# Retention followed by routed experts on one core: transposes spread between the products, and weight pieces issued ahead of the first scatter

## The chip, the cores and the metric

One core of a Trainium2 chip. The metric is the device time of one execution in microseconds; a run is one execution, and the figure for a kernel is the median of its runs.

## The reference

```python
# q, k, v: (4, 8, 768, 64); x has N = 3072 rows of D = 512; 8 experts, F = 1024
gamma = 1.0 - 2.0 ** (-5.0 - np.arange(H))
for t in range(S):
    state = gamma * state + einsum('bhd,bhe->bhde', k[:, :, t], v[:, :, t])
    y[:, :, t] = scale * einsum('bhd,bhde->bhe', q[:, :, t], state)
x = y.transpose(0, 2, 1, 3).reshape(N, D)

do_compute = x @ w_skip > 0          # rows that are not computed stay x
e_idx = argmax(xc @ w_gate)          # one expert for each row
gate_w = softmax(xc @ w_gate)[e_idx]
y[mask] = gate_w[mask] * (relu(xc[mask] @ w1[e]) @ w2[e])
out[do_compute] = xc + y
```

## The kernel before

Instructions run on each engine in the order in which the program writes them; the tile framework adds the waits. There are two stages.

**Attention.** The work is cut into 16 pairs, i = 0 to 15: one batch and two heads each. load(i) brings q, k and v of a pair (384 KB each) on SP's queue, three buffers for q and k, five for v. scaled_q and scaled_k multiply by powers of gamma on POOL. t_q and t_k transpose the scaled tiles on TensorE (six 128x128 transposes each), and ACT copies the result out of PSUM as QT and KT. s_at(i, r) forms the products of QT and KT for each half of the rows (24 small products), and DVE masks them into ATm. s_kv(i) forms k'v for each chunk (40 products), and DVE adds them up into the prefix sums Z. s_inter(i) multiplies QT by Z (20 products) and s_av(i) adds ATm times v (48 products) in the same PSUM tile; ACT copies it as xT. t_x(i) transposes it back (six transposes) into xall, and stores(i) writes finished rows to out on ACT's queue. One turn of the loop holds steps of different pairs: t_q(i+1), t_k(i+1), t_x(i-2), then s_inter(i-1), s_at(i, 0), s_kv(i), s_av(i-1), s_at(i, 1).

The PSUM tiles are: "P", two buffers of two banks, for t_q, s_at, t_x and all gate tiles; "KV", one buffer, for t_k and s_kv; "Y", one buffer, for s_inter and s_av.

Between these the router runs for a finished batch, one part in each turn: gates_pe(i) on TensorE (logits with the gate columns Wc; their transpose; counts; the table of slots) and gates_dve(i) on DVE (choice of the expert, values, positions, one-hot rows). Wc holds the gate's and the skip's columns; it is zeroed and then loaded by two small DMAs on SP.

The weights of the experts come as 64 pieces of 256 KB (fp32 in HBM, bf16 in SBUF), issued by POOL through give(n). Experts 0 to 3 are brought during the attention (list `quota`), experts 4 to 7 (32 pieces) afterwards, when the attention's memory is free.

**Experts.** A task is an expert and one or two tiles of 128 slots. gather brings the rows of a tile from out (indirect DMA on POOL), cast makes bf16 on DVE, turn transposes (four transposes) into xgT, layer1 runs 32 products with ACT's relu into hT, layer2 runs 8 products for each tile, DVE forms yo, and POOL scatters it to out. The first tiles of experts 0 to 3 can be gathered before the last batch is routed (SL[0]); the second tiles need SL[1]. Behind the head, ten tasks run in a loop: (2), (3), the second tiles of 0 to 3, then experts 4 to 7 with both tiles (n = 6 to 9). In turn n: layer1(n), turn(n+1), cast(n+2), layer2(n), gathers, give(3). A G_.drain() stands behind task n = 7. At the end a loop for experts with more than 256 rows runs npass times, here 0.

```python
    give(5)
    ha, pe = g_pick(g_turn(Gs))
    cast(0, [0])
    turn(0, [0])
    h0 = layer1(0, [0])
    cp = g_count(B - 1, ha)
    g_vals(B - 1, ha, pe)
    g_pos(B - 1, g_mine(ha, cp))
    cast(1, [0])
    turn(1, [0])
    layer2(0, h0, [0], SL, True)
    slot_table(one_hots(poolC, chunks(B - 1), [1]), chunks(B - 1), [1])
```

Of the kernel before, what the change touches and what calls it, by code (L numbers as in the profile page):

```python
# [9 lines left out]
FP32 = mybir.dt.float32  # L10
# [8 lines left out]
def kernel(  # L19
# [95 lines left out]
    def scaled_q(i, eng=G_):  # L115
        scaled(i, qs, qw, tq, "qs", 2, eng)
# [4 lines left out]
    for r in range(R):  # L121
        for hi in range(2):
            G_.affine_select(
                out=maskc[64 * hi : 64 * hi + 64, r, :], in_=maskc[64 * hi : 64 * hi + 64, r, :],
                pattern=[[1, C]], base=-r, channel_multiplier=-R, compare_op=ALU.is_ge, fill=0.0,
            )
    scaled_q(0, V_)
    scaled_k(0)
    load(2)

# [20 lines left out]
    def give(n):  # L151
        for _ in range(n):
            if pieces:
                piece_w(*pieces.pop(0))
# [15 lines left out]
    def t_k(i):  # L170
        if i >= NU:
            return
        KT[i] = poolR.tile([128, R, G, 128], FP32, tag="KT", bufs=2, name="KT")
        ps = psR.tile([128, 2, 512], FP32, tag="KV", bufs=1, name="ktps")
        turned(ps, ks[i])
        A_.copy(out=KT[i][:, :, :, :].rearrange("p r g t -> p r (g t)"), in_=ps[:, :, 0 : G * 128])
# [281 lines left out]
    def chunks(b):  # L458
        return list(range(b * NCH, (b + 1) * NCH))
# [31 lines left out]
    for i in range(NU + 1):  # L491
        scaled_q(i + 1)
        scaled_k(i + 1)
        if i == 0:
            s_at(0, 0)
            s_kv(0)
            s_at(0, 1)
            t_q(1)
            t_k(1)
        else:  # L500
            t_q(i + 1)
            t_k(i + 1)
            t_x(i - 2)
            stores(i)
            gates_pe(i)
            s_inter(i - 1)
            s_at(i, 0)
            s_kv(i)
            s_av(i - 1)
            s_at(i, 1)  # L510
            gates_dve(i)
        if i == 1:
# [27 lines left out]
            Wc = poolC.tile([128, NDB, 32], FP32, name="Wc")  # L540
            V_.memset(Wc[:, :, :], 0.0)
            with nc.allow_non_contiguous_dma(reason="gate columns"):
                SP.dma_start(out=Wc[:, :, 0:E], in_=moe_w_gate.rearrange("(a p) e -> p a e", p=128))
                SP.dma_start(out=Wc[:, :, E : E + 1], in_=moe_w_skip.rearrange("(a p o) -> p a o", p=128, o=1))
# [41 lines left out]
    def turn(e, sts):  # L586
        xgT[e] = poolE.tile([128, NDB, CAP], BF16, tag="xgT", bufs=3, name="xgT")
        for s in sts:
# [6 lines left out]
            V_.tensor_copy(  # L595
# [53 lines left out]
    give(5)  # L649
    psE = ctx.enter_context(tc.tile_pool(name="pse", bufs=1, space=bass.MemoryType.PSUM, reuse_waits="tile"))  # L650
    ha, pe = g_pick(g_turn(Gs))
    cast(0, [0])
    turn(0, [0])
    h0 = layer1(0, [0])
    cp = g_count(B - 1, ha)
    g_vals(B - 1, ha, pe)
    g_pos(B - 1, g_mine(ha, cp))
    cast(1, [0])
    turn(1, [0])
    layer2(0, h0, [0], SL, True)  # L660
    slot_table(one_hots(poolC, chunks(B - 1), [1]), chunks(B - 1), [1])
    SL[1] = slots(poolC, 1, "b")
    h0 = layer1(1, [0])
    cast(2, [0])
    turn(2, [0])
    layer2(1, h0, [0], SL, True)
    cast(3, [0])
    g_sum(B - 1, ha)
    cn = g_count_all()
    NPASS = (N + CAP - 1) // CAP - 1  # L670
    thr_i = poolC.tile([128, NPASS], I32, name="thr_i")
    G_.iota(thr_i[:, :], pattern=[[CAP, NPASS]], base=CAP, channel_multiplier=0)
    thr = poolC.tile([128, NPASS], FP32, name="thr")
    V_.tensor_copy(thr[:, :], thr_i[:, :])
    top = poolC.tile([128, 1], FP32, name="top")
    V_.tensor_reduce(out=top[:, :], in_=cn[:, 0, 0:E], axis=AXX, op=ALU.max)
    V_.tensor_scalar(thr[:, :], thr[:, :], top[:, 0:1], None, ALU.is_lt)
    npass = poolC.tile([128, 1], FP32, name="npass")
    V_.tensor_reduce(out=npass[:, :], in_=thr[:, :], axis=AXX, op=ALU.add)
    npass_i = poolC.tile([128, 1], I32, name="npass_i")  # L680
    V_.tensor_copy(npass_i[:, :], npass[:, :])
# [11 lines left out]
    for n, (e, sts) in enumerate(tasks):  # L693
# [8 lines left out]
        if n == len(tasks) - 3:  # L702
            G_.drain()
# [46 lines left out]
```

## Time and profile before

| | |
|---|---|
| median of 3 runs | 261.31 us (259.85 to 266.01) |
| the profiled execution | 260.44 us, span 258.7 us |
| PE busy | 202.4 us (78%), 3536 products |
| weight loads (PEld) busy | 161.9 us (63%) |
| DVE, ACT, POOL busy | 99.5, 77.3, 118.5 us |
| granted TensorE clock, mean | 0.94 |
| DMA moved | 49.83 MB, mean 193 GB/s |

The span runs from the first to the last instruction of the profiled execution; the time beside it has what lies around. Times in rows are microseconds from the span's start. Busy PE is not PE at its peak, since products are pipelined. In a timeline a row is a run of like instructions: its start, the time from the first's start to the last's end, the engine (an engine with q is its sequencer), the line, what is written and read, how many, and in brackets how long the engine had been idle before and what ended that. "issue" is idle time that the profile puts down to nothing that it shows.

### The profile page before, as it was taken

To read this page: it belongs to the slowest core of one execution; us is meant where nothing else is said; L and a number is where in the kernel's file an instruction comes from. 1 tells how busy PE (TensorE), PEld (TensorE's weight loads), DVE (VectorE), ACT (ScalarE), POOL (GpSimd) and SP (SyncE) were. 2 spreads that over 40 slices of the span, in tenths; PEclk is the share of its full clock that TensorE was granted. 3 is DMA by queue.
4 is the path that set the end of the run, shared out by engine and by line. 5 is a ranking of instruction groups with operands and counts; after the bars stand their busy time and mean duration, and the time that the engine had idled before them with its cause. 6 is when DMAs were issued, how large, how long until landed. Compare 5 with 4: busy or idle time off the path is not lost. (4 is left out here: it accounts for less than half of the span.)

```text
span 258.7 us, 8104 instructions
## 1 busy us (share of the span) xinstructions
PE 202.4 (78%) x3536; PEld 161.9 (63%) x3536; DVE 99.5 (38%) x304; ACT 77.3 (30%) x139; POOL 118.5 (46%) x146
## 2 busy tenths in 40 slices
PE   1899499977978966989795885887789999868080
PEld 1689389766877865879594763654457667626020
DVE  3135314334584243684135654344233514140020
ACT  2254144513522431543242222211224233303000
POOL 4672345552364165076290028013788787350411
PEclk9999979999999999999999998578999999997957
DMA  7991999969998988984989968920699999964611
GB/s 202 291 238 13 262 288 262 277 211 250 197 243 186 244 228 233 258 215 82 172 173 215 225 196 245 195 65 31 163 200 232 237 263 238 258 131 78 123 50 37
DMA packets 54520, 49.83 MB, mean 193 GB/s; under 512 B 3802, under 2 KB 42202, under 8 KB 54480
## 3 DMA queue, kind: packets, MB, share of 16 engines
q0 software_dynamic: 11776, 24.07, 46.4%
q1 hardware_dynamic: 38688, 18.90, 27.6%
q10 hardware_dynamic: 4016, 6.29, 6.9%
q8 instruction: 30, 0.49, 0.8%
q14 instruction: 10, 0.08, 0.1%
HBM read 56.64 MB, written 10.49 MB: 259 GB/s over the span
## 5 line engine op out<-in xcount | busy, mean ns | idle before, releaser
L207 DVE TENSOR_TENSOR ATm<-atps,maskc 128x768 f32<-128x768 f32 x32 | 30.6, 957 | 68.7 <-PE atps L203 62.6
L110 POOL TENSOR_TENSOR ks<-kw,tk 128x768 f32<-128x768 f32 x16 | 23.9, 1495 | 56.9 <-issue 49.6
L620 PE MATMUL yps<-w2b,hT 128*128 128x512 bf16 x128 | 35.3, 425 | 7.0 <-DMA w2b<-in_moe_w_dram 6.4
L608 PE MATMUL hps<-xgT,w1b 128*128 128x128 bf16 (+1 forms) x384 | 35.8, 253 | 6.1 <-DMA w1b<-in_moe_w_dram 3.1
L608 PEld LDWEIGHTS <-w1b 128*128 128x128 bf16 x384 | 30.6, 106 | 13.8 <-issue 6.0
L612 ACT ACTIVATE hT<-hps 128x256 bf16<-128x256 f32 (+1 forms) x48 | 21.4, 454 | 58.5 <-PE hps L608 48.8
L628 POOL DMA_INDIRECT out_dram<-yo,si x16 | 16.6, 1035 | 43.4 <-DVE yo L625 18.5
L203 PE MATMUL atps<-QT,KT 64*64 64x128 f32 x768 | 32.2, 278 | 2.4 <-issue 1.6
L262 PE MATMUL yps<-ATm,vw 64*64 64x128 f32 x768 | 27.3, 272 | 7.7 <-issue 7.4
L268 ACT COPY xT<-yps 128x768 f32<-128x768 f32 x16 | 12.8, 799 | 51.0 <-PE yps L262 48.9
L262 PEld LDWEIGHTS yps<-ATm,vw 64*64 64x64 f32 x768 | 22.2, 133 | 9.3 <-issue 8.8
L110 POOL TENSOR_TENSOR qs<-qw,tq 128x768 f32<-128x768 f32 x15 | 22.6, 1509 | 11.7 <-DMA qw<-in_q_dram 10.5
L620 PEld LDWEIGHTS <-hT 128*128 128x128 bf16 x128 | 13.1, 107 | 23.4 <-issue 13.4
L203 PEld LDWEIGHTS atps<-QT,KT 64*64 64x64 f32 x768 | 25.5, 136 | 3.2 <-issue 1.8
L142 POOL DMA_DIRECT2D w2b<-in_moe_w_dram x32 | 18.2, 580 | 16.1 <-issue 16.1
L165 PE MATMUL qtps<-ident,qs 128*128 128x128 f32 x96 | 14.8, 291 | 12.5 <-DVE qs L110 5.5
L625 DVE SCALAR_TENSOR_TENSOR yo<-yps,g,xg 128x512 f32<-128x512 f32 x16 | 11.8, 749 | 30.3 <-PE yps L620 29.7
L246 PE MATMUL yps<-QT,Z 64*64 64x128 f32 x320 | 21.5, 279 | 0.0
L184 ACT COPY QT<-qtps 128x768 f32<-128x768 f32 x16 | 13.8, 863 | 25.2 <-PE qtps L165 25.2
L165 PEld LDWEIGHTS qtps<-ident,qs 128*128 128x128 f32 x96 | 10.7, 146 | 15.4 <-issue 11.6
L569 POOL DMA_INDIRECT xg<-out_dram,gi x16 | 16.8, 1051 | 5.5 <-issue 4.6
L246 PEld LDWEIGHTS yps<-QT,Z 64*64 64x64 f32 x320 | 17.6, 136 | 2.6 <-issue 2.1
(99 smaller groups left out, 236.5 us busy)
## 6 DMA issues: line engine op xcount, KB each, us to landing
w1b<-in_moe_w_dram POOLq DMA_DIRECT2D x32, 256.0 KB
w2b<-in_moe_w_dram POOLq DMA_DIRECT2D x32, 256.0 KB
qw<-in_q_dram SPq DMA_DIRECT2D x16, 384.0 KB, 6.6
kw<-in_k_dram SPq DMA_DIRECT2D x16, 384.0 KB, 6.7
vw<-in_v_dram SPq DMA_DIRECT2D x16, 384.0 KB, 5.5
out_dram<-xall ACTq DMA_DIRECT2D x9, 512.0 KB, 6.6
out_dram<-xall ACTq DMA_DIRECT2D x1, 1152.0 KB
out_dram<-xall ACTq DMA_DIRECT2D x1, 384.0 KB, 5.1
```

Of the source, the lines that this page charges most:

```text
L110: eng.tensor_tensor(o[i][:, :, :, :], in_, sc, ALU.mult)
L142: G_.dma_start(out=w2b[e][:, 2 * a : 2 * a + 2, :].rearrange("p r d -> p (r d)"), in_=moe_w2[e, a * 256 : (a + 1) * 256, :].rearrange("(p ...
L165: PE.transpose(out=ps[:, r, g * 128 : (g + 1) * 128], in_=w[:, R * g + r, :, :].rearrange("p h d -> p (h d)"), identity=ident[:, :],)
L203: PE.matmul(out=ps[cp, h, g * C : (g + 1) * C], lhsT=KT[i][hp, r, g, cp], rhs=qcols(i, 2 * g + c)[hp], start=True, stop=True,)
L207: V_.tensor_tensor(out=ATm[i, r][:, :, :, :], in0=ps[:, :, 0 : G * C].rearrange("p h (g t) -> p h g t", g=G), in1=maskc[:, r, :].unsqueeze ...
L246: PE.matmul(out=Y[i][hp, c, g * C : (g + 1) * C], lhsT=Z[i][hp, ch - 1, :], rhs=qcols(i, ch)[hp], start=(ch <= 2), stop=False, skip_group_ ...
L262: PE.matmul(out=Y[i][64 * h : 64 * h + 64, c, g * C : (g + 1) * C], lhsT=vw[i][cp, h * G + g, r * D : (r + 1) * D], rhs=ATm[i, r][cp, h, g ...
L569: d = G_.indirect_dma_start(out=t[:, :], out_offset=None, in_=out[0:upto, :], in_offset=bass.IndirectOffsetOnAxis(ap=gi[:, e : e + 1], axi ...
L608: PE.matmul(out=hp[:, f, 0:n], lhsT=w1b[e][:, db, a * 256 + r : (a + 1) * 256 : 2], rhs=xgT[e][:, db, c0 : c0 + n], start=(db == 0), stop= ...
L612: A_.activation(out=hT[:, 2 * f2 : 2 * f2 + 2, 0:n], in_=hp[:, :, 0:n], func=AF.Relu, bias=0.0, scale=1.0)
L620: PE.matmul(out=yp[:, :], lhsT=hT[:, fb, n * 128 : (n + 1) * 128], rhs=w2b[e][:, fb, :], start=(fb == 0), stop=(fb == NFB - 1),)
L628: sc = G_.indirect_dma_start(out=out[:, :], out_offset=bass.IndirectOffsetOnAxis(ap=si[:, e : e + 1], axis=0), in_=yo[:, :], in_offset=Non ...
```

## The change

Four things are changed. Wc is zeroed on POOL at the head, and its two loads stand on SP behind load(2). Within a turn of the attention loop t_k, t_x, stores and gates_pe change places, s_av comes ahead of s_kv, and t_k takes its PSUM tile from "P". give(12) stands where give(5) stood. At the head of the experts cast(0) comes ahead of the gate, the first three xgT are copied by ACT, the slot table comes behind turn(2), and the count of passes moves into the loop (n = 2); the drain stands one task later.

```diff
+    Wc = poolC.tile([128, NDB, 32], FP32, name="Wc")
+    G_.memset(Wc[:, :, :], 0.0)
     scaled_q(0, V_)
     scaled_k(0)
     load(2)
+    with nc.allow_non_contiguous_dma(reason="gate columns"):
+        SP.dma_start(out=Wc[:, :, 0:E], in_=moe_w_gate.rearrange("(a p) e -> p a e", p=128))
+        SP.dma_start(out=Wc[:, :, E : E + 1], in_=moe_w_skip.rearrange("(a p o) -> p a o", p=128, o=1))
...
         KT[i] = poolR.tile([128, R, G, 128], FP32, tag="KT", bufs=2, name="KT")
-        ps = psR.tile([128, 2, 512], FP32, tag="KV", bufs=1, name="ktps")
+        ps = wide("ktps")
...
         else:
+            if i == NU:
+                gates_pe(i)
+                t_x(i - 2)
+                stores(i)
             t_q(i + 1)
-            t_k(i + 1)
-            t_x(i - 2)
-            stores(i)
-            gates_pe(i)
             s_inter(i - 1)
             s_at(i, 0)
-            s_kv(i)
+            t_k(i + 1)
             s_av(i - 1)
+            if i < NU:
+                t_x(i - 2)
+                stores(i)
+                s_kv(i)
+                gates_pe(i)
             s_at(i, 1)
             gates_dve(i)
         if i == 1:
...
-            Wc = poolC.tile([128, NDB, 32], FP32, name="Wc")
-            V_.memset(Wc[:, :, :], 0.0)
-            with nc.allow_non_contiguous_dma(reason="gate columns"):
-                SP.dma_start(out=Wc[:, :, 0:E], in_=moe_w_gate.rearrange("(a p) e -> p a e", p=128))
-                SP.dma_start(out=Wc[:, :, E : E + 1], in_=moe_w_skip.rearrange("(a p o) -> p a o", p=128, o=1))
...
-    def turn(e, sts):
+    def turn(e, sts, copy=V_.tensor_copy):
...
-            V_.tensor_copy(
+            copy(
                 xgT[e][:, :, s * 128 : (s + 1) * 128], pb[:, 0 : NDB * 128].rearrange("p (a t) -> p a t", a=NDB)
             )
...
-    give(5)
+    give(12)
     psE = ctx.enter_context(tc.tile_pool(name="pse", bufs=1, space=bass.MemoryType.PSUM, reuse_waits="tile"))
-    ha, pe = g_pick(g_turn(Gs))
     cast(0, [0])
-    turn(0, [0])
+    L = g_turn(Gs)
+    turn(0, [0], A_.copy)
+    ha, pe = g_pick(L)
     h0 = layer1(0, [0])
     cp = g_count(B - 1, ha)
+    pm = g_mine(ha, cp)
+    cast(1, [0])
+    turn(1, [0], A_.copy)
     g_vals(B - 1, ha, pe)
-    g_pos(B - 1, g_mine(ha, cp))
-    cast(1, [0])
-    turn(1, [0])
+    g_pos(B - 1, pm)
+    last = one_hots(poolC, chunks(B - 1), [1])
     layer2(0, h0, [0], SL, True)
-    slot_table(one_hots(poolC, chunks(B - 1), [1]), chunks(B - 1), [1])
+    cast(2, [0])
+    h0 = layer1(1, [0])
+    turn(2, [0], A_.copy)
+    slot_table(last, chunks(B - 1), [1])
+    layer2(1, h0, [0], SL, True)
     SL[1] = slots(poolC, 1, "b")
-    h0 = layer1(1, [0])
-    cast(2, [0])
-    turn(2, [0])
-    layer2(1, h0, [0], SL, True)
     cast(3, [0])
     g_sum(B - 1, ha)
-    cn = g_count_all()
...
+    def passes():
+        cn = g_count_all()
...
         give(3)
-        if n == len(tasks) - 3:
+        if n == 2:
+            passes()
+        if n == len(tasks) - 2:
             G_.drain()
```

## Rows read from the trace of the kernel before

**Rows 1.** Stages: length, busy time (count) by engine, PE clock, DMA share, GB/s.
```profile
40.00:60.00 20.00, 18.45 (x415) 16.27 (x406) 6.96 (x16) 9.00 (x14) 9.29 (x9) 1.00 0.96 249
...
172.00:187.00 15.00, 11.67 (x118) 7.96 (x116) 5.47 (x21) 3.75 (x11) 6.98 (x9) 0.89 0.35 100
...
206.00:230.00 24.00, 22.85 (x171) 15.60 (x170) 8.09 (x17) 7.16 (x12) 15.36 (x20) 1.00 1.01 235
230.00:252.00 22.00, 11.72 (x49) 5.77 (x47) 2.25 (x3) 2.39 (x4) 5.02 (x7) 0.77 0.46 89
```

**Rows 2.** Timeline of PE and of its weight loads, one pair.
```profile
40.50 0.87 PE L165 MATMUL qtps<-ident,qs 128*128 128x128 f32 x6
41.21 0.82 PE L165 MATMUL ktps<-ident,ks 128*128 128x128 f32 x6
41.87 0.82 PE L281 MATMUL xps<-ident,xT 128*128 128x128 f32 x6
42.62 1.19 PE L246 MATMUL yps<-QT,Z 64*64 64x128 f32 x17
...
47.17 0.87 PE L165 MATMUL qtps<-ident,qs 128*128 128x128 f32 x6
...
47.16 0.64 PEld L165 LDWEIGHTS qtps<-ident,qs 128*128 128x128 f32 x6 [0.17 <-issue]
```

**Rows 3.** Waits of PE up to 156 us: total, times, longest.
```profile
PE yps L262 <- issue: 7.4, 5, 2.4
...
PE cps L359 <- DVE ha L354: 1.2, 1, 1.2
```

**Rows 4.** Waits of SP's queue, and timeline, at pair 4.
```profile
SPq L77 <- PE yps L262: 53.4, 8, 9.4
SPq L543 <- DVE Tsb L548: 9.3, 1, 9.3
...
29.86 1.49 POOL L110 TENSOR_TENSOR qs<-qw,tq 128x768 f32<-128x768 f32 x1 [8.94 <-DMA qw<-in_q_dram]
...
31.41 0.87 PE L165 MATMUL qtps<-ident,qs 128*128 128x128 f32 x6 [3.45 <-POOL qs L110]
...
33.96 1.49 PE L281 MATMUL xps<-ident,xT 128*128 128x128 f32 x6
...
35.37 1.77 PE L246 MATMUL yps<-QT,Z 64*64 64x128 f32 x18
```

**Rows 5.** Timeline of PE at the head of the experts.
```profile
160.06 0.61 PE L592 MATMUL xtp<-identb,xb 128*128 128x128 bf16 x4 [2.24 <-DVE xb L584]
...
170.93 1.03 PE L429 MATMUL tabps<-rhsT,oh 128*128 128x40 bf16 x6 [1.09 <-DVE oh L421]
...
179.12 0.17 PE L406 MATMUL cnps<-Rsum,onesb 128*128 128x8 bf16 x1 [1.52 <-DVE Rsum L402]
```

**Rows 6.** Timeline of the last four tasks, PE and POOL.
```profile
206.16 3.69 PE L608 MATMUL hps<-xgT,w1b 128*128 128x256 bf16 x32
...
213.59 3.69 PE L608 MATMUL hps<-xgT,w1b 128*128 128x256 bf16 x32
...
233.55 5.01 PE L608 MATMUL hps<-xgT,w1b 128*128 128x256 bf16 x29 [3.14 <-DMA w1b<-in_moe_w_dram]
...
239.34 1.04 POOL L628 DMA_INDIRECT out_dram<-yo,si  x1 [8.58 <-issue]
...
241.69 1.18 POOL L142 DMA_DIRECT2D w2b<-in_moe_w_dram  x2
...
245.54 1.01 PE L620 MATMUL yps<-w2b,hT 128*128 128x512 bf16 x2 [6.12 <-DMA w2b<-in_moe_w_dram]
...
246.79 4.42 PE L620 MATMUL yps<-w2b,hT 128*128 128x512 bf16 x10 [0.24 <-DMA w2b<-in_moe_w_dram]
```

**Rows 7.** Timeline: a gather's issue, and the cast that waits for it.
```profile
208.16 1.06 POOL L569 DMA_INDIRECT xg<-out_dram,gi  x1 [0.30 <-issue]
...
214.60 0.43 DVE L584 CAST xb<-xg 128x512 bf16<-128x512 f32 x1 [3.40 <-DMA xg<-out_dram,gi]
```

More of the change, by code (lines that the diff above doesn't have):

```diff
@@ L668 @@
     g_sum(B - 1, ha)
-    cn = g_count_all()
     NPASS = (N + CAP - 1) // CAP - 1
[L671 to L677, printed above, removed]
@@ L678 @@
-    npass = poolC.tile([128, 1], FP32, name="npass")
-    V_.tensor_reduce(out=npass[:, :], in_=thr[:, :], axis=AXX, op=ALU.add)
-    npass_i = poolC.tile([128, 1], I32, name="npass_i")
-    V_.tensor_copy(npass_i[:, :], npass[:, :])
+    npass_i = poolC.tile([128, 1], I32, name="npass_i")
+    def passes():
+        cn = g_count_all()
+        thr_i = poolC.tile([128, NPASS], I32, name="thr_i")
+        G_.iota(thr_i[:, :], pattern=[[CAP, NPASS]], base=CAP, channel_multiplier=0)
+        thr = poolC.tile([128, NPASS], FP32, name="thr")
+        V_.tensor_copy(thr[:, :], thr_i[:, :])
+        top = poolC.tile([128, 1], FP32, name="top")
+        V_.tensor_reduce(out=top[:, :], in_=cn[:, 0, 0:E], axis=AXX, op=ALU.max)
+        V_.tensor_scalar(thr[:, :], thr[:, :], top[:, 0:1], None, ALU.is_lt)
+        npass = poolC.tile([128, 1], FP32, name="npass")
+        V_.tensor_reduce(out=npass[:, :], in_=thr[:, :], axis=AXX, op=ALU.add)
+        V_.tensor_copy(npass_i[:, :], npass[:, :])
```

## Prediction

> **What bounds the kernel now.** I read the table by stage first, then the waits of TensorE, then the timelines of three places. The chain that ended last is of no use here: it stops at the branch behind the last scatter. Four stages differ [rows 1]. In the attention loop (to about 155 us) PE is busy 18.45 of 20 us at granted clock 1.00, with the DMA engines at 0.96. Between 172 and 187 the experts start: PE 11.67 of 15 us, DMA only 0.35. From 206 to 230 both are full (22.85 of 24 us; DMA 1.01 at 235 GB/s). From 230 to 252 neither is: PE 11.72 of 22 us, DMA 0.46, clock 0.77. So there are holes at both ends of the experts, and the loop itself is full.
>
> In the loop one pair without gate work lasts from 40.50 to 47.17, 6.67 us, and PE goes from batch to batch without a gap [rows 2]. What breaks this are waits that the profile can put down to nobody ("issue"): 7.4 us in five stalls ahead of the s_av products alone, in the middle of a batch; beside it the longest wait for a gate is 1.2 us [rows 3].
>
> **Gate columns.** In the kernel before, SP's queue stood 9.3 us behind the two loads of Wc, which waited for DVE's memset, and the loads of pair 4 stood behind them. So POOL waited 8.94 us for q of pair 4, PE waited 3.45 us, and came back slower: t_x took 35.37 - 33.96 = 1.41 us against 0.75 [rows 2], and s_inter's 1.77 us row is 1.19 at speed [rows 2, 4]. Now POOL writes Wc at the head, where it waits for k anyway, and SP issues the two loads behind load(2). SP's other waits there are buffers that scaled_q and scaled_k free early. Worth: 3.45 + 0.66 + 0.58 and about 1 more for t_k between them = -5.7. It is safe in size between -3.5 (the wait alone) and -6.
>
> **Order of a pair.** No product is added. The eighteen transposes stood together; now t_k stands between s_at(i, 0) and s_av, t_x between s_av and s_kv. Each change between transposes and 64-wide products has a price: the t_k batch, inside the run, takes 41.87 - 41.21 = 0.66, t_x, with a change behind it, 0.75, t_q, with one ahead, 0.71; PE's weight loads stand idle 0.17 at such a change [rows 2]. One round trip costs between 0.05 + 0.09 = 0.14 and 2 x 0.17 = 0.34; I take 0.25, near the middle, as the weight load seen idle is partly covered by products that still run. There are two more per pair in 14 pairs: 28 x 0.25 = +7.0 (3.9 to 9.5).
> Against it stands the stall of 7.4 us [rows 3]. It falls inside a batch whose data are there, so I read it as PE's own supply of instructions, late while the DMA engines are full. If the supply sets the pace, bubbles of 0.25 us cost nothing, they only shorten the next stall; transposes (0.11 us each) spread among the quicker products also make PE use instructions at a steadier rate. I take back 5 of the 7.0. The gates move to the end of the pair: their waits, 1.2 us the longest, are then covered, but s_kv is late too, and DVE's chain of Z stands between PE and the two PSUM buffers ("P", now shared by six users, KT's transposes among them). I set these against each other at 0. At i = 16 the slot table stands ahead of t_x(14), which used to cover its one-hots: up to one t_x, +0.7. Sum of the order: +2.7, with -5 (stalls gone, switches free) and +9 (switches paid, stalls kept) as ends.
>
> **Head of the experts.** cast(0) now stands on DVE ahead of the gate; PE waited 2.24 us for it behind g_pick. The gather itself bounds what comes back: between 0 and 1.5, I take -1.2. cast(1) is moved ahead of g_vals and g_pos: -0.25. The slot table waited 1.09 us for its one-hots between layer2(0) and layer1(1); it moves behind turn(2), so -1.09, and its products then run warm, -0.4. g_count_all waited 1.52 us for Rsum ahead of the loop; in passes() it comes two tasks later, when Rsum is long there: -1.5 [rows 5]. xgT of the first three tasks is copied by ACT, which stands idle between its hT; priced at nothing, and if ACT is late by a copy, 0.6 each. SL[1] now comes behind layer2(1), but POOL's gathers wait for the scatter of that task anyway. Sum -4.5 (-7 to -1).
>
> **Twelve pieces.** This is the largest term. POOL's queue carries weight pieces, gathers and scatters in program order, and each task's three pieces stand behind its scatter. The last two pieces of expert 7 left at 241.69, behind a scatter that waited 8.58 us at the drain; PE waited for w1 until 233.55 and for w2 until 245.54 and 246.79 [rows 6]. Seven more pieces ahead move every later piece by 7/3 tasks, and the last goes out with n = 6 instead of n = 8. A piece of 256 KB at 235 GB/s takes 1.1 us; seven take 7.8, and the hole of 172 to 187 has 0.65 x 15 = 9.8 us free [rows 1], so they fit. Then every weight is there about 2.3 x 7.4 = 17 us earlier, at 216 to 230 on the old axis, ahead of its need. What is left is PE: tasks of two tiles start at 206.16 and 213.59, 7.43 apart [rows 6]. From 206.16 the last product ended at 246.79 + 4.42 = 251.21, 45.05 us; four tasks at 7.43 are 29.7, and I leave 1.5 for the last gather, whose cast PE met late: -13.9 (to -15.4 without that).
> The drain goes from ahead of the last two tasks to ahead of the last. If it again takes 8.6 us it ends some 2 us after the last yo is ready: 0 to +3, I take +1.
> Behind the twelve pieces (POOL 12 x 0.59 = 7 us [rows 6]) wait only the first two scatters, whose yo comes later than that.
>
> **Sum,** against the profiled execution of 260.4 us (span 258.7 and 1.7 around it; 0.9 below the median of 261.3): 260.4 - 5.7 + 2.7 - 4.5 - 13.9 + 1 = 240.0.
>
> **Rivals.**
> (1) The gathers pay for the pieces. All share POOL's software queue. In the full stretch a gather issued at 208.16 let its cast start at 214.60, 6.4 us later, behind the three pieces of the task before [rows 7]; seven new ones could hold up the gathers of the second rows and the last one. If pieces take 2 us each instead of 1.1, the seven take 14 us, not 7.8, where 9.8 are free; the 4.2 us over fall on the gathers, the head's gain is gone (+4.5) and the last gather is some 3 us later: 247. For it: DMA at 1.01 for 40 us. Against it: the hole.
> The Trainium skill (DMA: Bandwidth & Descriptors, "Queues, rings and completion order") says that a DMA engine consumes a ring in order and that the write which signals completion lands only after all earlier writes of that engine. By that rule this rival holds whenever the pieces are unfinished at the gather; the 6.4 us agree with it, and the chance below stands on those 6.4 us.
> (2) The supply of instructions is what the new order cures: the 7.4 us go and the switches vanish in what is left, -5 instead of +2.7: 232.
> (3) The columns bring nothing, since loads wait for buffers further on (SP's queue stands 53.4 us behind s_av's release of vw [rows 4]): the 5.7 are lost: 246.
> (4) Slower: the clock. The products now run in stretches of under 2.5 us between transposes. Behind its 3.45 us of waiting PE ran t_x at 1.41 against 0.75 and s_inter at 1.77 against 1.19, a factor of 1.5 to 1.9; a pair at that speed costs 6.67 x 0.65 = +4.3 us. Five such pairs take the gain back, seven give 270. Against it: the loop's clock is 1.00 [rows 1], though eighteen transposes stand together there.
> (5) The change does not bite: the pieces are held by the buffers that they reuse (stores of the last batch), and the tail stays: -13.9 and +1 gone, 253.
>
> **How the numbers follow.** Forecast 240 (236 to 245): 0.53. Rival 1: 0.17; rival 2: 0.13; rival 3: 0.07; rival 4: 0.04; rival 5: 0.06. The range of 8 in 10 is 230 to 250: rival 2 with the tail's full 15.4 below, rival 1 with the switches fully paid above; rivals 4 and 5 stay outside. 2%, about what a measurement of this kernel tells from no change, is 5.2 us, so faster by more means under 256: 0.92. Same 0.05 (two mishaps at once), slower 0.03 (the clock).
>
> **What would show it.** Columns: SP's wait for the Wc loads and PE's 3.45 us are gone. Order: weight loads idle 0.17 six times a pair, no batch of s_av stopped in the middle or as before. Head: no wait ahead of the slot table; layer1 of n = 0 about 4 us sooner after t_x(15). Pieces: DMA busy from 172 to 187; no wait of PE for w1b or w2b; the last four tasks 7.4 us apart. I am wrong if PE waits on KT or on DVE's masks in every pair, if casts wait for gathers over 3 us, or if the clock in the loop falls from 1.00.

## The result, and the profile after

The changed kernel takes 242.85 us (median of four runs, 241.57 to 243.84), the kernel before 261.44 (four runs, 259.85 to 266.01). The ratio is 0.932, with a 95% interval of 0.926 to 0.938. Ratios here leave out disturbed runs, those over 1.5% above the fastest of the same kernel: among them are eight of the ten with the columns alone, three of the four with the old order in the changed kernel and one without the last drain, and the profiles of these three kernels are of such a run.

The profiled execution took 242.13 us, span 240.4, against 260.44 and 258.7. Three marks on TensorE cut the difference of -18.3 us. The last s_av product ended at 154.19 and now ends at 149.37: -4.8. From there to the last product of the experts it took 97.0 us and now takes 82.9: -14.1. Behind the last product come 8.1 us instead of 7.5: +0.6. I made the forecast as -3.0, -18.4 and +1, in the same places. The total missed by 2.1 us, less than its parts: the experts gained 4.3 us less than I said, and in the loop two larger errors cancel.

First the table by stage, with the columns of [rows 1].

```profile
40.00:60.00 20.00, 20.00 (x472) 16.21 (x461) 6.88 (x19) 8.78 (x14) 7.96 (x7) 1.00 0.84 213
...
172.00:187.00 15.00, 10.04 (x96) 6.76 (x98) 4.11 (x8) 3.06 (x8) 10.45 (x14) 0.77 0.88 212
...
206.00:230.00 24.00, 23.79 (x176) 16.39 (x179) 8.03 (x16) 8.03 (x14) 10.21 (x12) 1.00 0.59 145
```

In this stretch of the loop PE has no holes any more (20.00 of 20 us); what is left of them up to 156 us follows below. The hole of the DMA engines at 172 to 187 is filled, 0.88 instead of 0.35, but it is now PE that stands there: 10.04 of 15 us, at a granted clock of 0.77. The end, 206 to 230, runs at 1.00 with the DMA engines at 0.59.

Next one pair on PE's timeline, the answer to [rows 2].

```profile
35.64 0.87 PE L172 MATMUL qtps<-ident,qs 128*128 128x128 f32 x6
36.45 1.19 PE L253 MATMUL yps<-QT,Z 64*64 64x128 f32 x17
...
38.34 0.87 PE L172 MATMUL ktps<-ident,ks 128*128 128x128 f32 x6
39.14 1.54 PE L269 MATMUL yps<-ATm,vw 64*64 64x128 f32 x48
40.62 0.87 PE L288 MATMUL xps<-ident,xT 128*128 128x128 f32 x6
41.42 0.85 PE L231 MATMUL kvps<-vw,ks 64*64 64x64 f32 x37
```

The next t_q starts at 42.92, so a pair takes 7.28 us; it took 6.67. Each of the three batches of transposes now takes 0.80 or 0.81 from its start to the next batch's; they took 0.71, 0.66 and 0.75 in a row. The pair's 0.61 us more is the price of two more round trips, 0.30 each. What it bought is in PE's waits, over the whole run (total, times, longest):

```profile
PE xtp L599 <- DVE xb L591: 7.9, 2, 7.2
...
PE hps L615 <- DVE xgT L602: 5.2, 1, 5.2
PE ktps L172 <- ACT seen L259: 2.2, 2, 1.1
...
PE kvps L231 <- issue: 1.4, 1, 1.4
```

The unnamed stalls are down to one of 1.4 us; there were 14.2 us of them before (7.4 at s_av [rows 3], 3.5 at t_q, and 3.3 at kvps and atps). No wait for w1b or w2b is left. Apart from the 5.4 us for the first q, which stood before too, the two longest waits are new, and both fall into the middle of the experts, on PE's timeline:

```profile
163.19 2.20 PE L615 MATMUL hps<-xgT,w1b 128*128 128x128 bf16 x32
...
176.74 0.61 PE L599 MATMUL xtp<-identb,xb 128*128 128x128 bf16 x4 [7.21 <-DVE xb L591]
...
193.38 3.45 PE L615 MATMUL hps<-xgT,w1b 128*128 128x128 bf16 x32 [5.19 <-DVE xgT L602]
...
202.82 3.69 PE L615 MATMUL hps<-xgT,w1b 128*128 128x256 bf16 x32
...
210.25 3.69 PE L615 MATMUL hps<-xgT,w1b 128*128 128x256 bf16 x32
...
228.62 3.62 PE L627 MATMUL yps<-w2b,hT 128*128 128x512 bf16 x15
```

Follow three stretches. From the end of s_av to layer1 of n = 0 it took 24.96 us and now takes 163.19 - 149.37 = 13.82: -11.1. From there to the first task of two tiles it took 27.0 (to 206.16 in [rows 6]) and now takes 39.63: +12.6. From there to the last product, 45.05 and now 29.4: -15.6; the tasks stand 7.43 apart to the end. So the head gained far more than I said, and the middle gave all of it back; of its 12.6 us, 7.21 and 5.19 are the two waits.

Of the head's 11.1 us, 4.3 are waits (PE idle 6.57 of 24.96 us before, 2.29 of 13.82 now) and 6.9 are products that take less time: the granted clock of this stretch was 0.73 and is 1.00. The first layer1 of the experts before,

```profile
161.19 3.57 PE L608 MATMUL hps<-xgT,w1b 128*128 128x128 bf16 x32 [0.52 <-DVE xgT L595]
```

and now:

```profile
154.06 2.13 PE L615 MATMUL hps<-xgT,w1b 128*128 128x128 bf16 x32 [1.07 <-ACT xgT L602]
```

At the end of the loop stands a third place, in the same view:

```profile
141.63 1.40 PE L436 MATMUL tabps<-rhsT,oh 128*128 128x40 bf16 x12 [1.51 <-DVE oh L428]
142.85 1.52 PE L288 MATMUL xps<-ident,xT 128*128 128x128 f32 x6
144.31 2.40 PE L253 MATMUL yps<-QT,Z 64*64 64x128 f32 x20
146.97 2.40 PE L269 MATMUL yps<-ATm,vw 64*64 64x128 f32 x48 [0.26 <-ACT seen L259]
```

Behind a stall of 1.43 us that ends at 137.63 and this wait for the one-hots PE runs slower; the granted clock is 0.56 from 140 to 150. In the kernel before, where it is 1.00, t_x takes 0.88 us, and the last two batches, behind a wait of 0.38 us, 1.31 and 1.54:

```profile
149.82 1.33 PE L429 MATMUL tabps<-rhsT,oh 128*128 128x40 bf16 x12 [0.38 <-DVE oh L421]
151.08 1.31 PE L246 MATMUL yps<-QT,Z 64*64 64x128 f32 x20
152.65 1.54 PE L262 MATMUL yps<-ATm,vw 64*64 64x128 f32 x48 [0.26 <-ACT seen L252]
```

What released the two waits of the middle stands in the timelines of POOL

```profile
153.31 2.24 POOL L147 DMA_DIRECT2D w1b<-in_moe_w_dram  x4
155.47 2.19 POOL L149 DMA_DIRECT2D w2b<-in_moe_w_dram  x4
159.97 0.53 POOL L147 DMA_DIRECT2D w1b<-in_moe_w_dram  x1 [2.31 <-DMA w1b<-in_moe_w_dram]
...
164.56 0.53 POOL L147 DMA_DIRECT2D w1b<-in_moe_w_dram  x1 [0.72 <-DMA w1b<-in_moe_w_dram]
...
169.02 1.04 POOL L576 DMA_INDIRECT xg<-out_dram,gi  x1 [0.30 <-issue]
...
191.84 0.23 POOL L687 IOTA thr_i<- 128x11 int32 x1
```

and of DVE:

```profile
159.94 0.75 DVE L632 SCALAR_TENSOR_TENSOR yo<-yps,g,xg 128x512 f32<-128x512 f32 x1
...
176.26 0.43 DVE L591 CAST xb<-xg 128x512 bf16<-128x512 f32 x1 [10.02 <-DMA xg<-out_dram,gi]
...
192.10 0.17 DVE L689 CAST thr<-thr_i 128x11 f32<-128x11 int32 x1 [7.13 <-POOL thr_i L687]
```

The first: POOL issues eight pieces without a pause and then, from the ninth on, waits ahead of each until an earlier one has landed (2.31, 1.54, 0.74 and 0.72 us). yo of the first task is ready at 160.69, but its scatter stands behind the twelfth piece, and the gathers of the second rows behind the scatters: 169.02. The first of them lands 7.2 us later, and the cast, and PE, wait for it. By the landings in the trace all of these come in the order of issue: the twelve pieces 1.2 to 2.1 us apart, the twelfth at 174.30, the scatters at 174.94 and 175.58, the gather at 176.23. The second: passes() issues its iota on POOL at n = 2. There it stands behind scatters, gathers and pieces until 191.84, and DVE waits 7.13 us for it, with the copy of xgT for task n = 4 queued behind; PE meets that wait ahead of layer1 at 193.38.

### The profile page after: what moved, and what is told of

Its sections match the earlier page's. It is cut to its first block, busy times and chain, and to the rows that moved or that the text cites. A ratio compares the mean times of both kernels' runs of the same rounds, so it can differ in the third digit from the quotient of the medians.

```text
span 240.4 us, 8071 instructions
## 1 busy us (share of the span) xinstructions
PE 200.1 (83%) x3526; PEld 157.8 (66%) x3536; DVE 102.5 (43%) x300; ACT 81.3 (34%) x142; POOL 118.4 (49%) x147
## 4 chain that ended last, share of the span: by engine, by line
PE 53%; DMA 12%; DVE 12%; issue 11%; POOL 6%; ACT 1%; POOLq 1%; SPq 0%; ACTq 0%; DVEq 0%
PE yps L269 8%; PE atps L210 8%; PE yps L253 7%; PE xps L288 6%; DMA w1b<-in_moe_w_dram 6%; PE kvps L231 6%; PE ktps L172 5%; PE qtps L172 4%; POOL out_dram L635 4%; PE gps L319 3%; DMA xg<-out_dram,gi 3%; DVE ATm L214 3%; PE hps L615 3%; PE yps L627 3%; DVE Z L243 2%
## 5 line engine op out<-in xcount | busy, mean ns | idle before, releaser
L615 PE MATMUL hps<-xgT,w1b 128*128 128x128 bf16 (+1 forms) x384 | 33.0, 244 | 6.8 <-DVE xgT L602 5.2
L615 PEld LDWEIGHTS <-w1b 128*128 128x128 bf16 x384 | 29.2, 102 | 11.9 <-issue 7.9
L627 PE MATMUL yps<-w2b,hT 128*128 128x512 bf16 x118 | 29.7, 391 | 0.5
L635 POOL DMA_INDIRECT out_dram<-yo,si x16 | 16.3, 1021 | 26.2 <-DVE yo L632 15.8
L210 PEld LDWEIGHTS atps<-QT,KT 64*64 64x64 f32 x768 | 24.0, 135 | 3.1 <-ACT KT L183 1.3
L269 PE MATMUL yps<-ATm,vw 64*64 64x128 f32 x768 | 25.5, 280 | 0.3 <-ACT seen L259 0.3
L253 PE MATMUL yps<-QT,Z 64*64 64x128 f32 x320 | 22.2, 283 | 0.0
L627 PEld LDWEIGHTS <-hT 128*128 128x128 bf16 x128 | 12.4, 101 | 13.1 <-issue 1.6
L147 POOL DMA_DIRECT2D w1b<-in_moe_w_dram x32 | 17.8, 571 | 5.3 <-DMA w1b<-in_moe_w_dram 5.3
L253 PEld LDWEIGHTS yps<-QT,Z 64*64 64x64 f32 x320 | 18.3, 138 | 2.7 <-issue 2.2
L241 DVE COPY Z<-kvps 128x64 f32<-128x64 f32 x16 | 3.6, 224 | 36.6 <-PE kvps L231 36.6
L183 ACT COPY KT<-ktps 128x768 f32<-128x768 f32 x16 | 12.8, 799 | 18.9 <-PE ktps L172 18.9
```

What stands on the lines that cost most here:

```text
L147: G_.dma_start(out=w1b[e][:, a, :], in_=moe_w1[e, a * 128 : (a + 1) * 128, :])
L210: PE.matmul(out=ps[cp, h, g * C : (g + 1) * C], lhsT=KT[i][hp, r, g, cp], rhs=qcols(i, 2 * g + c)[hp], start=True, stop=True,)
L253: PE.matmul(out=Y[i][hp, c, g * C : (g + 1) * C], lhsT=Z[i][hp, ch - 1, :], rhs=qcols(i, ch)[hp], start=(ch <= 2), stop=False, skip_group_ ...
L269: PE.matmul(out=Y[i][64 * h : 64 * h + 64, c, g * C : (g + 1) * C], lhsT=vw[i][cp, h * G + g, r * D : (r + 1) * D], rhs=ATm[i, r][cp, h, g ...
L615: PE.matmul(out=hp[:, f, 0:n], lhsT=w1b[e][:, db, a * 256 + r : (a + 1) * 256 : 2], rhs=xgT[e][:, db, c0 : c0 + n], start=(db == 0), stop= ...
L627: PE.matmul(out=yp[:, :], lhsT=hT[:, fb, n * 128 : (n + 1) * 128], rhs=w2b[e][:, fb, :], start=(fb == 0), stop=(fb == NFB - 1),)
```

## The experiments

Marks of the profiled executions, worked out from each trace, one execution each: t_q(6) is the start of pair 6's q transposes, stalls are PE's unnamed waits from 40 to 156 us, the experts last from the end of the last s_av to the last product. The end of s_av moves between executions too: the kernels before, with the drain moved and with twelve pieces have the same loop and end it at 154.19, 157.10 and 161.07; the changed loop ends at 148.31 to 153.80 in seven. So a difference of a few us at that mark between two lines may be the execution's.

```
                                     t_q(6)  s_av end  stalls  experts  behind it
before                                47.17    154.19    14.2     97.0        7.5
+ columns only                        47.39    154.91    13.9     98.5        7.4
+ order only                          46.06    152.37     2.4     94.1        7.6
+ drain moved only                    47.41    157.10    12.9     88.1        7.6
+ twelve pieces only                  49.09    161.07     9.4     82.8        8.1
+ no weights of experts 0-3 loaded    48.53    144.63     1.8     95.8        7.6
changed                               42.92    149.37     1.4     82.9        8.1
 with the old order                   46.57    158.41    15.8     83.1        8.1
 with five pieces                     46.12    152.12     2.0     83.1        7.6
 with the drain early                 45.40    150.81     1.2     82.8        7.3
 with the iota early                  44.07    150.00     2.4     81.7        8.1
 with iota early, five pieces         43.86    148.31     1.1     80.8        7.2
 with iota early, eight pieces        46.18    153.80     3.4     76.5       10.1
 iota early, five, no last drain      45.52    151.84     1.9     81.7       13.5
```

**The gate columns alone.** In the kernel before:

```
+    Wc = poolC.tile(...); G_.memset(Wc[:, :, :], 0.0)
     scaled_q(0, V_); scaled_k(0); load(2)
+    SP.dma_start(Wc, gate); SP.dma_start(Wc, skip)
...
-            Wc = ...; V_.memset(...); SP.dma_start(...) x2      (at i == 1)
```

> The kernel before with the gate columns of the change alone. Theory (loads held up once): SP's 9.3 us behind the Wc loads go, POOL's 8.94 us wait for q of pair 4 and PE's 3.45 us with its slow batches go: 261.4 - 5 = 256 (255 to 257); PE's stalls with no named cause inside batches stay near 14 us in all. Rival (the lead in loads is what freed PE of those stalls too): PE's unnamed stalls fall under 4 us, 261.4 - 5 - 10 = 246 to 249. Second rival (loads wait for buffers anyway): 260 to 262.

Measured: 261.91 us, median of ten runs (253.19 to 264.46); before 261.6 on the same chip (259.43 to 265.07). The two runs that the ratio counts, 253.19 and 256.5, give 0.976 (0.968 to 0.984), about the 255 to 257 of the theory; the other eight, 260.16 to 264.46, lie where the kernel before lies. So whether the columns alone bring 6 us or nothing is not settled. The profile is of one of the eight (262.63 us) and tells why nothing came of it in that run, on PE's timeline:

```profile
28.38 0.87 PE L170 MATMUL qtps<-ident,qs 128*128 128x128 f32 x6
...
37.07 0.33 PE L267 MATMUL yps<-ATm,vw 64*64 64x128 f32 x2 [2.54 <-issue]
...
38.48 1.54 PE L170 MATMUL qtps<-ident,qs 128*128 128x128 f32 x6
...
45.16 0.27 PE L229 MATMUL kvps<-vw,ks 64*64 64x64 f32 x2 [0.80 <-issue]
...
47.39 0.88 PE L170 MATMUL qtps<-ident,qs 128*128 128x128 f32 x6
```

t_q(4) starts at 28.38 without a wait, 3.0 us sooner than in [rows 4]. The loads run ahead (DMA share 1.16 from 15 to 25 us, where it was 0.43), and then an unnamed stall of 2.54 us comes, behind which t_q runs at 1.54 us instead of 0.87. At t_q(6) the lead is gone: 47.39 against 47.17.

**The order alone.** The loop order and KT in the shared buffer, as in the diff of the change, and nothing else.

> The kernel before with the order of the loop alone (KT's transposes in the shared PSUM buffers too). Theory (order pays for itself): unnamed stalls of PE fall from about 14 to under 4 us, -11, two more changes between transposes and products in each of 14 pairs at 0.3 us and the waits on the PSUM buffers at the gates give +9 to +11 back: 259 to 263. Rival (the stalls went with the gate columns, the order only costs): stalls stay, 261.4 + 9 = 268 to 272. Second rival (the order is worth more than it costs since its bubbles lie inside stalls): 254 to 258.

Measured: 257.48 us (255.78 to 259.71), ratio 0.986 (0.975 to 0.998). Stalls of 2.4 us; the end of s_av 1.8 us earlier; the wait for w2b at the end stands (8.3 us). So the order is worth about 4 us, by the ratio's interval 0.7 to 6.5, and not a cost of 2.7, as the second rival of the expectation has it. Of the 4.6 us by which the profiled runs differ, 2.9 lie in the experts, which the order does not touch.

**The old order in the changed kernel.**

```
-            if i == NU: gates_pe(i); t_x(i - 2); stores(i)
-            t_q(i + 1); s_inter(i - 1); s_at(i, 0); t_k(i + 1); s_av(i - 1)
-            if i < NU: t_x(i - 2); stores(i); s_kv(i); gates_pe(i)
+            t_q(i + 1); t_k(i + 1); t_x(i - 2); stores(i); gates_pe(i)
+            s_inter(i - 1); s_at(i, 0); s_kv(i); s_av(i - 1)
-        ps = wide("ktps")
+        ps = psR.tile([128, 2, 512], FP32, tag="KV", bufs=1, name="ktps")
```

> The changed kernel with the old order of a pair. Theory (the order ends the unnamed stalls, and the columns are worth something only once these are gone): unnamed stalls of 12 to 16 us again, last logits at 154 to 156 us instead of 149.4, and the time 247 to 250. Rival (a loop that ends later is absorbed, since the second rows' gathers set the pace of the first experts): 243 to 245 in spite of stalls. The prediction's own sum, in which the order costs 2.7 us, gives 240.

Measured: 251.38 us, median of four runs (246.28 to 252.84), against 241.57 to 243.84 with the new order. Stalls of 15.8 us are back, as the theory has it, in a profile of 251.46 us. By the lowest run alone, the only one that a ratio would count, the order is worth 2.4 to 4.7 us here, less than the theory's price of 4 to 7; the size is not settled. The sign rests on all four runs, which lie above all four of the changed kernel.

**Are the stalls a matter of transfers?** In the kernel before, the 32 weight pieces of experts 0 to 3 are not loaded; POOL writes zeros in their place, so the experts compute something else.

```
 def piece_w(e, which, a):
+    if e < NEARLY:
+        if which == 0:
+            G_.memset(w1b[e][:, a, :], 0.0)
+        else:
+            G_.memset(w2b[e][:, 2 * a : 2 * a + 2, :], 0.0)
+        return
```

> The kernel before, in which the weights of experts 0 to 3 are not loaded: POOL writes zeros into each of those pieces where it issued the transfer, so the output is not the reference's, and all else stands. Theory (PE's stalls that have no name are its supply of instructions, late where the DMA engines are full): with some third of the transfers of the loop gone the DMA share of 40 to 60 us falls from 0.96 to 0.55 to 0.75, the unnamed stalls of PE to 155 us fall from 14 us to under 5, and the last batch's logits end at 146 to 150 us instead of 154.2. Rival (the stalls belong to the program, to its order of products and the semaphores between them): the stalls stay at 11 to 16 us, with the same spacing, and the logits end at 153 to 155. Only the loop is read; the experts compute with zeros.

Measured: 249.31 us (248.12 to 250.52), ratio 0.958 (0.943 to 0.973). Stretches of it, with the columns of [rows 1],

```profile
60.00:100.00 40.00, 35.87 (x900) 32.36 (x897) 22.64 (x62) 14.57 (x25) 23.19 (x20) 1.00 0.66 193
100.00:140.00 40.00, 35.78 (x908) 32.12 (x906) 25.06 (x77) 15.42 (x27) 24.06 (x24) 1.00 0.29 93
```

and PE's groups from 20 to 156 us (count, busy and mean of one, idle before by releaser):

```profile
L268 PE MATMUL yps<-ATm,vw 64*64 64x128 f32 x768 | 25.8, 272 | 1.2 <-issue 0.9 <-ACT seen L258 0.3
...
L171 PE MATMUL qtps<-ident,qs 128*128 128x128 f32 x78 | 12.3, 294 | 4.5 <-POOL qs L110 3.6 <-issue 0.9
```

With the DMA share at 0.66 and 0.29, where the kernel before has 0.93 and 0.86, the stalls fall from 14.2 to 1.8 us in the old order, the same instructions on PE, and s_av ends 9.6 us earlier. So the old order stalls only beside the transfers; the new one does not stall much beside them either. What PE waits for is its instructions, as their packets show (last section). The run also gives the price of the new order: from t_q(6) to the end of s_av it takes 106.5 us in the changed kernel, 96.1 here, almost without stalls and in the old order, 107.0 in the kernel before. In these three executions ten us are paid to be rid of eleven. Over all of them the old loop takes 107.0, 109.7 and 112.0 us (before, drain moved, twelve pieces), the new order 104.5 to 107.6 in seven.

**The drain alone.** In the kernel before:

```
-        if n == len(tasks) - 3:
+        if n == len(tasks) - 2:
             G_.drain()
```

> The kernel before with the drain alone moved, from behind the last task but two (n = 7) to behind the last but one (n = 8); still 5 pieces ahead of the first scatter. Theory (the drain, not the number of pieces, held the last weights back: POOL stood 8.58 us there with two pieces of w2 still to issue): PE's waits for w1b and w2b in the last task fall from 9.5 us to 3 or 4, 261.4 - 8 = 253 (251 to 256). Rival (the prediction's: the pieces come too late because too few went ahead): the last two pieces are issued behind the scatters of n = 8 all the same, PE still waits 7 us or more for weights, 259 to 262.

Measured: 254.7 us (252.74 to 256.1), ratio 0.973 (0.963 to 0.983), though its loop ended 2.9 us later in the profile. PE's waits for weights:

```profile
PE yps L620 <- DMA w2b<-in_moe_w_dram: 2.8, 2, 1.7
...
PE hps L608 <- DMA w1b<-in_moe_w_dram: 1.4, 1, 1.4
```

They were 3.14 and 6.36 us in [rows 6]. So with five pieces ahead it was the drain's place that held the last pieces back, two tasks from the end, and one moved line brings 8.9 us in the experts; 4.2 us of waits for weights stay.

**Twelve pieces alone.** In the kernel before, give(5) becomes give(12).

> The kernel before with twelve pieces ahead instead of five, nothing else. The prediction's term of 13.9 us gives 247 to 249. Theory (the pieces repair the end, because all are out before the drain, and give part of it back at the gathers of the second rows): PE waits for w1b and w2b under 2 us in all, PE waits of 4 us or more for the casts of the second rows, time 251 to 255. Rival (the gathers pay for all of it): 258 or more.

Measured: 252.37 us (251.26 to 255.93), ratio 0.967 (0.949 to 0.985). The experts take 82.8 us, 14.2 less than before: my term of 13.9, by itself, with the drain in its old place. The loop of this execution ended 6.9 us later, ahead of anything that the edit touches (t_q(6) is already 1.9 late, and the granted clock was 0.92 from 60 to 100 us), so the run's time shows less. POOL's timeline shows why the gathers don't pay here:

```profile
175.50 0.53 POOL L140 DMA_DIRECT2D w1b<-in_moe_w_dram  x1 [1.01 <-DMA w1b<-in_moe_w_dram]
...
184.60 1.02 POOL L628 DMA_INDIRECT out_dram<-yo,si  x1 [6.25 <-DVE yo L625]
...
185.96 1.06 POOL L569 DMA_INDIRECT xg<-out_dram,gi  x1 [0.17 <-issue]
```

The twelfth piece is out at 175.50, and the second scatter waits 6.25 us for its yo: the old head is so slow that the pieces are gone before a gather could leave. PE's waits for the casts are 4.4 us in three, none over 2.1, less than expected above.

**Five pieces, or the early drain, in the changed kernel.**

> The changed kernel with 5 pieces ahead of the first scatter instead of 12. Theory (twelve pieces win the tail but hold up POOL and the gathers of the second rows): PE's 7.2 us wait for the cast in n = 0 falls under 2, POOL does not wait for a landed piece ahead of its first scatter, but the last weights come late again: PE waits 6 to 14 us for w1b and w2b in the last task; 242.9 - 6 + 11 = 248 (244 to 253). Rival (the pieces cost the head nothing): the wait of 7.2 us stays and the tail's 15.6 us are lost: 255 to 259.

> The changed kernel with the drain put back behind the last task but two; 12 pieces ahead. Theory: with 12 ahead all pieces are out before that drain, so no weight is late and only scatters of n = 8 wait: 242.9 + 0 (241 to 245). Rival (the drain's place alone makes the tail): 249 to 253, with waits of PE in the last two tasks.

Measured: 244.02 us (242.84 to 245.55) with give(5), 242.04 (240.44 to 243.68) with the drain back at len(tasks) - 3. In the experts five pieces cost 0.2 us and the early drain nothing. With the two before this is nearly a table of two by two: five and early 97.0, five and late 88.1 or, in the new head, 83.1; twelve and early 82.8 in either head, twelve and late 82.9 in the new one. Five and early with the new head, and twelve and late with the old one, were not run. Either remedy repairs the end in whole or for the larger part; in the new head the second brings nothing on top. The expectation of 248 us for five pieces, with 6 to 14 of waits for weights, was too dear: these waits are 3.1 us. With five pieces the gathers of the second rows come in time, but the iota is then the wait (PE, total, times, longest):

```profile
PE hps L615 <- DVE xgT L602: 8.6, 1, 8.6
...
PE xtp L599 <- DVE xb L591: 0.9, 2, 0.7
```

**The iota among the constants,** alone and with five pieces. In the changed kernel the iota of thr_i moves from passes() to the head of the program.

> The changed kernel with the small iota of the pass count written among the constants at the head instead of in POOL's queue behind the pieces of n = 2. Theory (DVE waited 7.13 us for POOL's queue, and PE 5.2 us for DVE's copy of xgT, then ran slow): those waits go, n = 3 starts 5 us sooner and at full clock: 242.9 - 6 = 237 (235 to 239). Rival (DVE would have waited for a gather there anyway): a cast waits instead, 241 to 243.

> The changed kernel with the iota of the pass count among the constants and 5 pieces ahead instead of 12. Theory (two things stall the tasks n = 0 to 3: the gathers behind twelve pieces, 7.2 us, and DVE behind POOL's iota, 5 to 9 us; each hides the other): both waits go, tasks 4 us apart from n = 0 on, PE waits 3 us for weights at the end: 235 (233 to 237). Rival (whatever is saved in the middle is waited for at the end, since the transfers set the pace): 239 to 242, with waits for w1b and w2b over 6 us.

Measured: 241.5 us (238.5 to 242.04) with twelve pieces and 240.01 (238.08 to 241.78) with five; ratios to before 0.922 (0.913 to 0.931) and 0.920 (0.912 to 0.928). In both the wait of 5.2 us is gone, and little of it shows: with twelve pieces the casts' waits grow from 7.9 to 10.4 us, with five they are 5.4 and the weights come late again (w1b 1.5, w2b 1.9). From 172 to 206 us the DMA share is 1.0 to 1.1 with five pieces. I read this as the transfers of that stretch, which have to be made: what one place in POOL's queue saves another pays. No run took them out there.

**Eight pieces,** as many as POOL issued without waiting.

> The changed kernel with the iota of the pass thresholds among the constants and eight pieces ahead instead of twelve. Theory (POOL stands only from the ninth unfinished piece on, so eight leave the gathers of the second rows on time and still bring all weights ahead of need): PE waits for the casts of the second rows under 3 us, for weights under 1.5 us, time 236 to 239. Rival (the transfers of the stretch from 170 to 210 us set the pace, and what one queue position saves another loses): 239.5 to 242, as with five or twelve.

Measured: 241.27 us (240.29 to 243.21), ratio 0.928 (0.910 to 0.946); the theory's 236 to 239 did not come. The waits came as the theory has them (PE, total, times, longest):

```profile
PE xtp L603 <- DVE xb L595: 2.5, 2, 1.8
...
PE yps L631 <- DMA w2b<-in_moe_w_dram: 0.7, 1, 0.7
```

and the experts took 76.5 us, the shortest of all. The time did not: s_av ended 4.4 us later than in the changed kernel, with stalls of 3.4 us, and 10.1 us came behind the last product. The loop is the same in both, so I put its 4.4 us down to the execution; whether the 10.1 belong to the kernel stays open. It can't be told from the changed kernel by its time.

**Without the last drain,** otherwise as iota early with five pieces.

> As the kernel with the early iota and 5 pieces ahead, and without the drain ahead of the last task. Theory (the drain holds the last task's scatters back some 2 us: 8.43 us from its issue behind the last pieces): 1.5 to 2.5 us below that kernel. Rival (what POOL waits for there is the transfers themselves, drain or not): same within 0.7 us.

Measured: 244.37 us (243.03 to 248.85), slower by 4 and not faster by 2, as the theory had it. In the profile, of the run of 248.85 us, the last scatter is issued at

```profile
234.62 1.02 POOL L639 DMA_INDIRECT out_dram<-yo,si  x1 [1.70 <-DVEq L724]
```

and the span ends at 247.1; with the drain, the last scatter is at 230.22 and the span ends at 236.3. So 11.5 us instead of 5 lie behind the last scatter's issue. I read it so that what must settle there is settled by the drain while PE still works; the profile does not say what it is, and the other three runs, some 4 to 6 us shorter, have none. The ratio to before is 0.932 (0.924 to 0.941), against 0.920 with it.

## Why the prediction was right, and where its steps failed

The forecast of 240.0 lies 2.1 us under the profiled run, partly by luck: 12.6 us in the middle of the experts, which I had not counted, stand against 6.6 more than forecast in the head, 1.7 in the last four tasks and 1.8 in the loop. Two of the signs that I had set for being wrong came, casts that wait over 3 us (7.2) and a clock in the loop under 1.00 (0.56 from 140 to 150 us).

**Gate columns, -5.7.** The mechanism is right: SP no longer stands behind the Wc loads, POOL waits 0.86 us for q of pair 4 instead of 8.94, and PE's 3.45 us are gone. The size isn't shown. From t_q(3) to t_q(6) it takes 21.92 us instead of 25.94, with three pairs that are each 0.61 longer: -5.8. But with the order alone the same stretch takes 23.91, and the other six executions with both take 21.85 to 24.35, so next to the order the columns are worth 2.1 us there or less. What I missed is that the gain lasts only if the stalls go: in the profiled run with the columns alone it was gone by t_q(6), behind a stall that came as the loads ran ahead. Its two lowest runs have no profile.

**Order of a pair, +2.7.** This step failed, in its sign. From t_q(6) to the end of s_av, some ten pairs, its terms are these. The switches were 0.61 a pair, 6.1 there, and 8.5 for 14 pairs, where I took 7.0: right in kind, inside the range. "I take back 5 of the 7.0" was the error: 12.8 us of stalls went. I had counted only the five at s_av and let the switches fill them; those at t_q, kvps and atps had the same cause. "I set these against each other at 0", of the gates, was wrong the other way: t_k and t_q now wait 4.9 us for the shared PSUM buffers behind the gates (ACT seen 2.2, DVE's pm, L and Tsb 2.7), while 2.6 us of waits for the gates went (ha 1.2, sm 0.6, oh 0.8). And i = 16, "+0.7", cost about 3.7: 1.51 - 0.38 of waiting for the one-hots, which t_x no longer covers, and 2.6 for three batches at the low clock. Together that is -0.7, and the stretch measures -0.6 (106.45 against 107.03). The kernel before was the best of three executions of its loop, and the time of the order alone says -4, so -0.6 is the low end. Of my rivals the second happened in part: the stalls were cured, but the switches did not vanish. Whether the third (columns bring nothing) would have happened without the order is open. The sum of columns and order, -4.8, is near my -3.0 by luck.

**Head, -4.5, and the first rival.** The head gained 11.1 us, more than twice that. Its waits gave 4.3, about the 4.0 that I had summed; the term that was mis-sized is the clock, "its products then run warm, -0.4", which gave 6.9, with a granted clock of 1.00 instead of 0.73 over the head (0.89 from 172 to 187 in [rows 1]). None of it reached the end, since the experts take 82.9 us with the new head and 82.8 with the old one and twelve pieces. The first rival's mechanism took it, as I had it at 0.17: the gathers of the second rows pay for the pieces, because with the new head the first yo is ready (160.69) before the pieces are out (165.09). "Behind the twelve pieces wait only the first two scatters, whose yo comes later than that" is the sentence that failed. I had priced the twelve issues at 7 us of POOL's time; from 153.31 to 165.09 they took 11.8, as POOL waits for landed pieces from the ninth on. The Trainium skill (DMA: Bandwidth & Descriptors, "Queues, rings and completion order") says that the write which signals a completion lands only after all earlier writes of that DMA engine; the trace agrees with it: the gather issued at 169.02 landed at 176.23, behind the twelfth piece and the scatters, 7.2 us; it was 6.4 in [rows 7]. The wait for the iota, 5.2 us, was in no rival. I had read passes() as a move of DVE's work to a place where Rsum is ready, and did not count that it also issues on POOL, in a queue where every entry waits its turn.

**Twelve pieces, -13.9.** The size is right: -14.2 alone, -15.6 from the first task of two tiles on. The reason is only half right: I gave it to the number of pieces ahead, and the drain's place alone repairs 8.9 of it. In the changed kernel, where the drain is late anyway, five or twelve makes 0.2 us.

**Drain, +1.** Behind the last product it cost 0.6 us; with the drain put back there are 7.3 us there instead of 8.1. My view of it as a cost alone was too narrow: without it the kernel with the early iota and five pieces is 4 us slower.

The other rivals did not decide: the clock (rival 4) stays at 1.00 or 0.98 in the loop until 140 us and costs its 2.6 us in the last pair alone, and the tail went (rival 5).

## What to carry to other kernels

When an engine stops in the middle of a batch and the profile names nobody, take transfers out and look again: here that moved 14.2 us of stalls to 1.8. Then look at when the packets of instructions arrive. Here a change of order and a change of transfers each ended the stalls. Edits that pull work forward don't add up where one queue carries everything: price them in one table of two by two, and follow each new entry of that queue to what stands behind it, down to an iota of 0.23 us. A drain or any wait for completion holds back what is issued behind it: here its place alone was worth 8.9 us of the 14.2 that more transfers ahead of it brought. And read a mark from more than one execution: the same loop ended up to 6.9 us apart.

## What the runs showed of the chip

PE's unnamed stalls in the kernel before come a fixed number of products apart. On its timeline, where a row starts when the stall ends,

```profile
56.88 0.87 PE L203 MATMUL atps<-QT,KT 64*64 64x128 f32 x20 [1.55 <-issue]
...
64.65 1.43 PE L262 MATMUL yps<-ATm,vw 64*64 64x128 f32 x43 [1.82 <-issue]
...
76.11 0.55 PE L165 MATMUL qtps<-ident,qs 128*128 128x128 f32 x3 [1.42 <-issue]
...
82.50 1.10 PE L262 MATMUL yps<-ATm,vw 64*64 64x128 f32 x32 [1.18 <-issue]
```

there are 126, 254 and 127 products between them, and 254, 126, 508, 254 and 127 between the next ones, so about 127 or a multiple of it, with as many weight loads. The queue of kind instruction moved 30 packets and 0.49 MB in that run, 16 KB each; 254 instructions in 16 KB would be 64 bytes each, an estimate from these two numbers. So instructions seem to come in blocks, by the same engines as the data.

The times of these packets in the trace show that the stalls are waits for them. The last one ahead of each of the four rows ended at 55.28, 63.24, 74.78 and 81.14, and PE went on 1.60, 1.42, 1.33 and 1.36 us later. The packets come some 6 us apart, yet in all 14 kernels each of the 68 unnamed stalls of more than 0.3 us between 15 and 156 us ended 1.07 to 1.61 us behind the end of one. The trace does not have when a packet was asked for, so how long each queued is not shown.

The Trainium skill (DMA: Bandwidth & Descriptors, "Queues, rings and completion order") states that a DMA engine goes round the queues that have work, a packet at a time; a block of instructions would then take turns with packets of data, which agrees with the stalls leaving when the DMA share fell to 0.66. Why the new order loses the stalls at about the same DMA share (0.97 from 60 to 100 us, 0.93 before) wasn't tried. Counted in blocks of 127 products from 40 to 140 us, PE took 3.4 to 7.5 us for a block in the old order without the 32 pieces and 5.1 to 7.5 in the changed kernel; that more even blocks are what ends the stalls is only argued.

POOL waits ahead of the ninth piece that has not landed, here and with twelve pieces in the kernel before (0.99 to 1.48 us each there). In the changed kernel the first four pieces landed at 159.69, 161.75, 163.03 and 164.27, and the ninth to twelfth were issued 0.28 or 0.29 us behind that. Whether that is a limit of the queue or of the semaphores that the program uses can't be told from the traces.
